# Memory products of two heads in either half of TensorE's rows, with the norm in the same stationary tile

## The chip, the cores and the metric

One core of a Trainium2 chip runs the whole program. The metric is device time in microseconds, from start to end of one execution; lower is better. The kernel before was run three times: 965.25, 966.20 and 967.39 us, median 966.2 us.

## What is computed

Three blocks follow one another: attention with a memory term, and two feed-forward blocks on its output. B = 4, H = 8, S = 576, D = 64; there are 2304 tokens of 512 features. The change concerns the memory term, `mem_ret` and `mem_norm`:

```python
def _attn_ref(q, k, v, M_prev, z_prev, beta):
    scores = scale * np.matmul(q, k.transpose(0, 1, 3, 2))
    ...
    local = np.matmul(a, v)
    q_p = phi(q)                      # where(x > 0, x, exp(x) - 1) + 1
    mem_ret = np.einsum('bhsd,bhde->bhse', q_p, M_prev)
    mem_norm = np.einsum('bhsd,bhd->bhs', q_p, z_prev)[..., None] + 1e-06
    mem_out = mem_ret / mem_norm
    g = 1.0 / (1.0 + np.exp(-beta))[None, :, None, None]
    return g * mem_out + (1 - g) * local

x = moe(attention)    # ((x @ w1) * (x @ w2)) @ w3 @ w_out
out = moe2(x)         # h = x @ w_in; (h * tanh(softplus(h))) @ w_out
```

## The kernel before

**Tasks.** Heads are taken in pairs. A `Task` is one pair of one batch, for one half (288 queries) of the sequence or for both. Batch 0 is split (eight tasks of one half each), batches 1 to 3 have four tasks of two halves each: 20 tasks, 32 halves. The first twelve (`AVF=12`) do the memory term and the product with V in float32, one `matmul` of which becomes two passes on TensorE. The last eight use float32r: a number is split into a high part and a low part and the product is the sum of three one-pass products, in the order of `HL = ((0, 0), (0, 1), (1, 0))`. So 16 halves are float32 and 16 are float32r.

**Stages of a task.** `load_qk` and `prep` bring K and Q of a head and split them (tile `QK`); `phi` makes the features of both heads, head 0 in partitions 0 to 63 and head 1 in 64 to 127 (tile `PH`). `load_vm` brings V and the memory. `SC` makes the scores on TensorE, finds their maxima with DVE and POOL; `SE` subtracts and takes the exponent. `MEM` makes the memory products, `AV` the products with V. At the end of the second head's `AV` the denominators are gathered by small DMAs through DRAM into `cp` so that 128 partitions can work on them, added to an epsilon, inverted, multiplied with the gate, sent back and broadcast into `Rr`, with which DVE multiplies `mnl`.

**The memory products before** (`MEM`, line 503). The stationary tile is 128 x 128, block-diagonal: M of head 0 in the upper left, M of head 1 in the lower right, so that one product over 128 rows gives both heads' outputs in 128 partitions. The two norm vectors are two more columns (`VZ = P + 2`) and a product of their own into a second PSUM bank, with 2 rows of output in float32 and 4 in float32r (high and low part of the vectors are columns beside one another; the two rows are added later). One ACT copy takes the outputs to `mnl`, one takes the norm rows to `R`:

```python
op("pe", cost, fm, r=rd, w=[pm])
act(HS, lambda qs=qs: mnl.tile[:, 0, qs], lambda pm=pm: pm.tile[:, 0:HS], [pm], [(mnl, (0, hf))], True)
op("pe", cost, fn, r=rd, w=[pn])
act(HS, lambda qs=qs, nz=nz: R.tile[0:nz, qs], ...)
```

**The norms of float32r tasks** (`AV`, line 647). The low rows of `R` go by a third DMA to DRAM, come back into a tile `cz`, and DVE adds them to `cp`.

**Who sets the order.** Every operation is recorded with an engine, a cost in ns and what it reads and writes (`op`, line 82). At the end `schedule` (line 111) lists them: each engine takes, when it is free in the planned time, the ready operation with the lowest key, for TensorE the place in the program (filler work 300 places later), for the others the longest remaining path. The result is one fixed order for each engine, which on the chip waits on semaphores only. Products of the first feed-forward block fill TensorE between attention steps (names `x`, `u`, `wA` to `wE`); the second feed-forward block comes after them. PSUM is eight banks, all with the name `g`. Lines 330, 333, 337, 339 and 347 are helpers (`mm`, `sub`, two forms of `act`, `tt`) and occur in rows of many tiles; DMAs are issued by the SP queue at line 327.

Of the kernel before, what the change touches and what calls it, by code (L numbers as in the profile page):

```python
# [14 lines left out]
P = 128  # L15
# [247 lines left out]
def kernel(  # L263
# [28 lines left out]
    VZ = P + 2  # L292
# [21 lines left out]
        "x": 10, "u": 4, "t": 8, "cp": 1, "cz": 2, **CFG.get("BUFS", {}),  # L314
# [126 lines left out]
    def load_vm(T):  # L441
        j = T.nj
        n = 2 * j * DV
        if T.f32:
            M = T.M = buf("M", [P, VZ])
            dma(lambda: Vf.tile[:, T.i % 2, 0:j], lambda: v[T.b, T.p, :, 0:j], 512 * n, w=[(Vf, T.i % 2)])
            dma(lambda: M.tile, lambda: mz[T.b, T.p], 66560, w=[M])
            return
        raw = buf("vr", [P, VZ + 2 * NJ * DV])
        mr = lambda: raw.tile[:, 0:VZ]  # L450
        vr = lambda: raw.tile[:, VZ:VZ + n].rearrange("p (j t d) -> p j t d", t=2, d=DV)
        dma(vr, lambda: v[T.b, T.p, :, 0:j], 512 * n, w=[(raw, 0)])
        dma(mr, lambda: mz[T.b, T.p], 66560, w=[(raw, 1)])

        M = T.M = buf("M", [P, 2 * VZ], F32R)
        act(VZ, lambda: M.tile[:, 0:VZ], mr, [(raw, 1)], [(M, 0)])
        for a, b, c in ((0, P, VZ + 2), (P, VZ, VZ)):
            lo(b - a, lambda a=a, b=b, c=c: M.tile[:, c:c + b - a], lambda a=a, b=b: mr()[:, a:b], lambda a=a, b=b: M.tile[:, a:b], [(raw, 1), (M, 0)], [(M, 1)])
# [44 lines left out]
    def MEM(T):  # L503
        T.mnl = buf("mnl", [P, 2, T.w])
        T.R = buf("R", [P, T.w])
        PH, mnl, R, M = T.PH, T.mnl, T.R, T.M
        for hf in T.hfs:
            pm, pn = gbuf(), gbuf()
            qs = T.qs(HS * hf, HS * hf + HS)
            if T.f32:  # L510
                rd, cost, nz = [PH, M], 2 * 248, 2
                fm = lambda pm=pm, qs=qs: mm(pm.tile[:, 0:HS], M.tile[:, 0:P], PH.tile[:, qs], True, True)
                fn = lambda pn=pn, qs=qs: mm(pn.tile[0:2, 0:HS], M.tile[:, P:VZ], PH.tile[:, qs], True, True)
            else:
                rd, cost, nz = [(z, y) for z in (PH, M) for y in range(2)], 3 * t_mm(HS), 4

                def fm(pm=pm, qs=qs):
                    for y, (a, b) in enumerate(HL):
                        mm(pm.tile[:, 0:HS], M.tile[:, (VZ + 2) * a:(VZ + 2) * a + P], PH.tile[:, b, qs], y == 0, y == 2)

                def fn(pn=pn, qs=qs):
                    mm(pn.tile[0:4, 0:HS], M.tile[:, P:VZ + 2], PH.tile[:, 0, qs], True, False)
                    mm(pn.tile[0:4, 0:HS], M.tile[:, P:VZ + 2], PH.tile[:, 1, qs], False, True)
# [80 lines left out]
    def AV(T, t):  # L604
# [35 lines left out]
        d0 = Buf(dram, [6, W], F32, f"d0_{W}", 2)  # L640
# [3 lines left out]
        dma(lambda: d0.tile[0:2], lambda: R.tile[0:2, :], 9216, r=[(R, (2, hf)) for hf in T.hfs], w=[(d0, 0)])  # L644
        dma(lambda: d0.tile[2:4], lambda: R.tile[32:65:32, :], 9216, r=[(R, (x, z)) for x in range(2) for z in range(len(T.outs))], w=[(d0, 1)])
        dma(lambda: cp.tile, lambda: d0.tile[0:4].rearrange("r (c e) -> (r c) e", e=ce), 9216, r=[(d0, 0), (d0, 1)], w=[(cp, 0)])
        if not T.f32:
            dma(lambda: d0.tile[4:6], lambda: R.tile[2:4, :], 9216, r=[(R, (2, hf)) for hf in T.hfs], w=[(d0, 2)])
            cz = buf("cz", [64, ce])
# [397 lines left out]
```

## Time and profile before

| | |
|---|---|
| median of three runs | 966.2 us |
| profiled execution: its time / its span | 965.84 us / 964.1 us |
| PE busy | 945.7 us (98%), 5440 matmul instructions |
| DVE busy | 725.8 us (75%), 1643 instructions |
| ACT busy | 607.0 us (63%), 1240 instructions |
| DMA queue | 31.3% of 16 engines |
| TensorE clock granted | 1.00, in every slice |

Busy time of PE includes the tail of each pipelined matmul, which lies beside the next one: how long a group of matmuls holds TensorE is read from its start to the start of what follows. The memory products stand between 6.7 and 431 us. From about 460 us on there is no attention left, only feed-forward products.

### The profile page before, as it was taken

Reading aid. Unit: us, or ns where it says so; the run is one execution under the profiler, and the core shown is the slowest. Engines: PE = TensorE matmul, PEld = TensorE weight load, DVE = VectorE, ACT = ScalarE, POOL = GpSimd, SP = SyncE. Lnnn points to the kernel's source line nnn. Section 1 sums busy time; section 2 is a strip of 40 time slices with the busy share of each in tenths; the row PEclk is TensorE's granted clock in tenths of the full one; section 3 lists DMA queues with packets and bytes.
Section 4 is the critical chain, followed back from the end, with each engine's and each line's share of the span. In section 5 each row is a group of like instructions: output and inputs, shape, how many; then the busy total and the mean of one; then the engine's idle time right before and its main releaser. Section 6 shows DMA issues by size and latency. Waiting matters only on the chain.

```text
span 964.1 us, 15222 instructions
## 1 busy us (share of the span) xinstructions
PE 945.7 (98%) x5440; PEld 808.9 (84%) x5440; DVE 725.8 (75%) x1643; ACT 607.0 (63%) x1240; POOL 86.4 (9%) x70
## 2 busy tenths in 40 slices
PE   6999999999999999999999999999999999999998
PEld 3454878778999999999999988888888888998997
DVE  7999999899999989896653987547554756565663
ACT  6677877778797778775433776446444544554653
POOL 1210012322222012120000000000000000000000
PEclk9999999999999999999999999999999999999999
DMA  9689655542433422302641740020002001100000
GB/s 351 215 246 303 201 167 153 156 141 82 142 98 91 151 75 83 107 26 83 203 153 49 228 167 1 1 81 7 1 1 83 1 0 32 46 1 17 34 1 33
DMA packets 48316, 96.62 MB, mean 100 GB/s; under 512 B 11024, under 2 KB 23344, under 8 KB 48240
## 3 DMA queue, kind: packets, MB, share of 16 engines
q1 hardware_dynamic: 48240, 95.64, 31.3%
q8 instruction: 43, 0.70, 0.3%
q14 instruction: 33, 0.27, 0.1%
HBM read 85.85 MB, written 9.77 MB: 99 GB/s over the span
## 4 chain that ended last, share of the span: by engine, by line
PE 67%; DVE 18%; ACT 6%; DMA 4%; issue 3%; SPq 1%; POOL 0%; DVEq 0%; ACTq 0%; POOLq 0%
PE g L330 67%; DVE t L347 4%; DVE QK L333 3%; DMA Rr<-d 2%; DVE e L333 1%; DVE e L347 1%; ACT t L339 1%; DVE mnl L347 1%; DVE g L560 1%; SPq L327 1%; DVE u L333 1%; DVE t L686 1%; ACT mnl L337 1%; DMA wA<-in_moe_w_out_dram 1%; ACT R L337 1%
## 5 line engine op out<-in xcount | busy, mean ns | idle before, releaser
L330 PE MATMUL g<-u,wA 128*128 128x288 f32 (+2 forms) x1008 | 162.6, 314 | 1.0 <-ACT u L337 0.6
L330 PEld LDWEIGHTS g<-u,wA 128*128 128x128 f32 x1008 | 147.2, 188 | 9.9 <-ACT u L337 1.0
L347 DVE TENSOR_TENSOR t<-g,t 128x288 f32<-128x288 f32 (+6 forms) x344 | 121.3, 380 | 22.2 <-PE g L330 14.4
L580 POOL PARTITION_ALL_REDUCE t<-t x64 | 85.8, 1342 | 352.0 <-DVE t L347 282.5
L330 PE MATMUL g<-x,wB 128*128 128x288 f32 x768 | 110.7, 298 | 0.8 <-DVE t L347 0.8
L330 PEld LDWEIGHTS g<-x,wB 128*128 128x128 f32 x768 | 104.7, 188 | 3.3 <-DVE t L347 1.4
L339 ACT ACTIVATE x<-x,two 128x512 f32<-128x512 f32 (+1 forms) x80 | 54.4, 680 | 70.8 <-DVE x L830 70.8
L339 ACT ACTIVATE x<-g 128x512 f32<-128x512 f32 (+1 forms) x98 | 55.0, 561 | 65.2 <-PE g L330 63.9
L330 PE MATMUL g<-e,V 128*65 128x320 f32 (+12 forms) x576 | 90.3, 303 | 1.9 <-ACT e L339 1.5
L833 DVE SCALAR_TENSOR_TENSOR x<-g,x 128x512 f32<-128x512 f32 (+1 forms) x80 | 51.0, 637 | 43.0 <-ACT x L339 42.6
L330 PEld LDWEIGHTS g<-e,V 128*65 128x65 f32 (+1 forms) x576 | 66.2, 136 | 20.3 <-ACT e L339 3.0
L829 DVE TENSOR_SCALAR x<-x 128x512 f32<-128x512 f32 (+1 forms) x80 | 31.8, 397 | 61.8 <-ACT x L339 60.0
L330 PE MATMUL g<-QK 128*128 128x320 f32 (+7 forms) x464 | 72.8, 298 | 5.2 <-DVE QK L333 5.1
L337 ACT CAST x<-x 128x512 fp32r<-128x512 f32 (+1 forms) x80 | 46.1, 577 | 50.4 <-DVE x L347 50.3
L330 PEld LDWEIGHTS g<-QK 128*128 128x128 f32 x464 | 64.0, 193 | 14.8 <-DVE QK L333 7.8
L333 DVE TENSOR_TENSOR t<-x 128x512 fp32r<-128x512 f32 (+1 forms) x80 | 50.9, 637 | 31.9 <-ACT x L337 30.6
L330 PE MATMUL g<-wB,wD 128*128 128x512 f32 x128 | 61.6, 619 | 3.9 <-DVE wD L686 2.1
L333 DVE TENSOR_TENSOR QK<-ld,QK 64x640 fp32r<-64x640 f32 (+1 forms) x80 | 61.7, 772 | 3.5 <-ACT QK L337 1.9
L330 PE MATMUL g<-x,wD 128*128 128x288 f32 x384 | 57.0, 298 | 0.0
L337 ACT COPY t<-g 128x288 f32<-128x288 f32 (+2 forms) x96 | 36.5, 394 | 32.5 <-PE g L330 24.7
L330 PE MATMUL g<-x,wE 128*128 128x288 f32 x384 | 56.2, 300 | 0.5 <-DVE e L347 0.4
L347 DVE TENSOR_TENSOR x<-x 128x512 f32<-128x512 f32 (+1 forms) x80 | 51.0, 637 | 6.0
(147 smaller groups left out, 1815.6 us busy)
## 6 DMA issues: line engine op xcount, KB each, us to landing
ld<-in_qk_dram SPq DMA_DIRECT2D x24, 608.0 KB
u<-in_moe_w_dram SPq DMA_DIRECT2D x26, 512.0 KB
Rr<-d SPq DMA_DIRECT2D x24, 288.0 KB
mnl<-in_moe_w_out_dram SPq DMA_DIRECT2D x11, 512.0 KB
mnl<-in_moe_w_in_dram SPq DMA_DIRECT2D x11, 512.0 KB
x2d<-t SPq DMA_DIRECT2D x16, 288.0 KB
out_dram<-x SPq DMA_DIRECT2D x18, 256.0 KB
wA<-in_moe_w_out_dram SPq DMA_DIRECT2D x8, 512.0 KB
```

Of the source, the lines that this page charges most:

```text
L327: op("sp", max(500, nbytes / 340.0), lambda: nc.sync.dma_start(out=dst(), in_=src()), r, w)
L330: nc.tensor.matmul(out=o, lhsT=lhsT, rhs=rhs, start=start, stop=stop)
L333: eng.tensor_tensor(out=o, in0=a, in1=b, op=ALU.subtract)
L337: op("act", t_act(n, psum), lambda: nc.scalar.copy(out=o(), in_=i()), r, w)
L339: op("act", t_act(n, psum), lambda: nc.scalar.activation(out=o(), in_=i(), func=func, **kw), r, w)
L347: op(eng, t_dve(n) if eng == "dve" else t_pool(n), lambda: e.tensor_tensor(out=o(), in0=a(), in1=b(), op=alu), r, w)
L560: nc.vector.tensor_tensor(out=o, in0=o, in1=mv, op=ALU.add)
L580: op("pool", 430 + 2.6 * (b - a), lambda mv=mv: nc.gpsimd.partition_all_reduce(mv(), mv(), P, bass_isa.ReduceOp.max), r=[(m, x)], w=[(m, x)])
L686: op("dve", t_dve(512), lambda: nc.vector.scalar_tensor_tensor(out=ci(), in0=ci(), scalar=3, in1=lw(), op0=ALU.logical_shift_left, op1=ALU ...
L829: op("dve", t_dve(n, True), lambda: nc.vector.tensor_scalar(out=w_(), in0=u(), scalar1=E20, scalar2=2.0, op0=ALU.min, op1=ALU.add), r=[ub_ ...
L833: op("dve", t_dve(n), lambda: nc.vector.scalar_tensor_tensor(out=u(), in0=hv(), scalar=2.0 ** -8, in1=u(), op0=ALU.mult, op1=ALU.mult), r= ...
```

## The change

The stationary tile of a head is now its own 64 partitions: 64 columns of M, and in the other 64 columns one column with its norm vector and zeros. Head 0 has M in columns 0 to 63 and z in column 64; head 1 has z in column 0 and M in columns 64 to 127. A half is one operation on TensorE with two PSUM banks, one for each head; head 0's product uses partitions 0 to 63 of `M` and `PH`, head 1's partitions 64 to 127, in turns over the passes. Outputs and norm of a head come out in one bank, and four ACT copies take them out: two of 64 x 288 to `mnl`, two of 1 x 288 to `R`, head 0's norm to row 0 and head 1's to row 96. In float32r tasks the low part of the norm is inside the three products, so the third DMA, `cz` and its addition are gone, as is the separate splitting of the two norm columns.

```diff
@@ load_vm
-            M = T.M = buf("M", [P, VZ])
+            M = T.M = buf("M", [P, P])
...
-        for a, b, c in ((0, P, VZ + 2), (P, VZ, VZ)):
-            lo(b - a, lambda a=a, b=b, c=c: M.tile[:, c:c + b - a], ...)
+        lo(P, lambda: M.tile[:, 1], mr, lambda: M.tile[:, 0], [(raw, 1), (M, 0)], [(M, 1)])
@@ MEM
-            pm, pn = gbuf(), gbuf()
+            pt = [gbuf(), gbuf()]
-            if T.f32:
-                rd, cost, nz = [PH, M], 2 * 248, 2
-                fm = lambda pm=pm, qs=qs: mm(pm.tile[:, 0:HS], M.tile[:, 0:P], PH.tile[:, qs], True, True)
-                fn = lambda pn=pn, qs=qs: mm(pn.tile[0:2, 0:HS], M.tile[:, P:VZ], PH.tile[:, qs], True, True)
-            else:
-                rd, cost, nz = [(z, y) for z in (PH, M) for y in range(2)], 3 * t_mm(HS), 4
...
-            op("pe", cost, fm, r=rd, w=[pm])
-            act(HS, lambda qs=qs: mnl.tile[:, 0, qs], lambda pm=pm: pm.tile[:, 0:HS], [pm], [(mnl, (0, hf))], True)
-            op("pe", cost, fn, r=rd, w=[pn])
-            act(HS, lambda qs=qs, nz=nz: R.tile[0:nz, qs], lambda pn=pn, nz=nz: pn.tile[0:nz, 0:HS], [pn], [(R, (2, hf))], True)
+            passes = [(None, None)] if T.f32 else HL
+            def fm(pt=pt, qs=qs):
+                for y, (a, b) in enumerate(passes):
+                    for t, r in enumerate(HALF):
+                        w, x = (M.tile[r], PH.tile[r, qs]) if T.f32 else (M.tile[r, a], PH.tile[r, b, qs])
+                        mm(pt[t].tile[:, 0:HS], w, x, y == 0, y == len(passes) - 1)
+            op("pe", 2 * 248 if T.f32 else 3 * t_mm(HS), fm, ..., w=pt)
+            for t, ps in enumerate(pt):
+                act(HS, lambda qs=qs, r=HALF[t]: mnl.tile[r, 0, qs], lambda ps=ps, r=HALF[t]: ps.tile[r, 0:HS], ...)
+                act(HS, lambda qs=qs, r=96 * t: R.tile[r:r + 1, qs], lambda ps=ps, r=64 - 64 * t: ps.tile[r:r + 1, 0:HS], ...)
@@ AV
-        dma(lambda: d0.tile[0:2], lambda: R.tile[0:2, :], 9216, ...)
+        dma(lambda: d0.tile[0:2], lambda: R.tile[0:97:96, :], 9216, ...)
...
-        if not T.f32:
-            dma(lambda: d0.tile[4:6], lambda: R.tile[2:4, :], 9216, ...)
-            cz = buf("cz", [64, ce])
-            dma(lambda: cz.tile, ..., 9216, r=[(d0, 2)], w=[cz])
-            op("dve", 90, lambda: nc.vector.tensor_tensor(out=cp.tile[0:64], in0=cp.tile[0:64], in1=cz.tile, op=ALU.add), ...)
```

The planned cost of a half on TensorE falls from two times 496 to 496 ns in float32, and from two times `3 * t_mm(HS)` to one in float32r, and ACT's planned work grows, so the fixed orders shift a little on every engine. They stay close: the attention steps keep their sequence, and the filler products before each of them are the same within a few.

On TensorE, in a float32 task, between filler products (`wB,wD`) and the next head's scores (`QK`; `e` with `V` are the products with V). Before:

```order
L330 MATMUL g<-wB,wD 128x512 x2
L330 MATMUL g<-PH,M 128x288
L330 MATMUL g<-PH,M 2x288
L330 MATMUL g<-QK 128x288 x2
L330 MATMUL g<-QK 128x160 x2
```

and with the change:

```order
L329 MATMUL g<-wB,wD 128x512 x2
L329 MATMUL g<-PH,M 128x288 x2
L329 MATMUL g<-QK 128x288 x2
L329 MATMUL g<-QK 128x160 x2
L329 MATMUL g<-QK 128x32 x2
```

The place is the same. In place of the outputs' product and the norms' product stand two products over 64 rows each, one for each head.

On TensorE, in a float32r task of two halves, between products of the feed-forward block (`u,wA`) and the next head's scores. Before:

```order
L330 MATMUL g<-u,wA 128x288 x48
L330 MATMUL g<-PH,M 128x288 x3
L330 MATMUL g<-PH,M 4x288 x2
L330 MATMUL g<-PH,M 128x288 x3
L330 MATMUL g<-PH,M 4x288 x2
L330 MATMUL g<-QK 128x256 x2
```

and with the change:

```order
L329 MATMUL g<-u,wA 128x288 x48
L329 MATMUL g<-PH,M 128x288 x12
L329 MATMUL g<-QK 128x256 x2
L329 MATMUL g<-QK 128x128 x2
L329 MATMUL g<-QK 128x320 x2
```

Ten products have become twelve, each over 64 rows, head 0 and head 1 in turns.

On ACT, the copies out of PSUM of one float32r task of two halves, with what stands behind them. Before:

```order
L337 COPY t<-g 128x288
L337 COPY mnl<-g 128x288
L337 COPY R<-g 4x288
L337 COPY mnl<-g 128x288
L337 COPY R<-g 4x288
L337 CAST PH<-t 128x576
L337 CAST M<-vr 128x130
L337 COPY t<-g 128x256
```

and with the change:

```order
L336 COPY mnl<-g 64x288
L336 COPY R<-g 1x288
L336 COPY mnl<-g 64x288
L336 COPY R<-g 1x288
L336 COPY mnl<-g 64x288
L336 COPY t<-g 128x256
L336 COPY R<-g 1x288
L336 COPY mnl<-g 64x288
L336 COPY R<-g 1x288
L336 COPY t<-g 128x320
L336 CAST QK<-ld 128x1216
L336 CAST PH<-t 128x576
```

Four copies have become eight. The copies of the next scores (`t<-g`) now stand between them, and the conversion of `QK` and that of `PH` for the next task behind them.

## Rows read from the trace of the kernel before

**Rows 1.** The page: span, busy time of each engine, chain of waits by engine.

```profile
span 964.1 us, 15222 instructions
PE 945.7 (98%) x5440; PEld 808.9 (84%) x5440; DVE 725.8 (75%) x1643; ACT 607.0 (63%) x1240; POOL 86.4 (9%) x70
...
PE 67%; DVE 18%; ACT 6%; DMA 4%; issue 3%; SPq 1%; POOL 0%; DVEq 0%; ACTq 0%; POOLq 0%
```

**Rows 2.** Four stretches: us, then busy us (x instructions) of each engine, clock, DMA.

```profile
0.00:50.00 50.00, 40.04 (x134) 20.52 (x135) 42.89 (x125) 31.79 (x62) 8.65 (x12) 1.00 0.79 280
50.00:215.00 165.00, 162.72 (x891) 118.28 (x889) 156.75 (x409) 125.05 (x274) 31.93 (x24) 1.00 0.63 196
215.00:450.00 235.00, 232.66 (x1779) 224.44 (x1779) 213.07 (x543) 183.09 (x424) 45.87 (x34) 1.00 0.32 95
450.00:964.00 514.00, 510.32 (x2643) 445.64 (x2641) 313.04 (x567) 267.02 (x482) 0.00 (x0) 1.00 0.17 54
```

**Rows 3.** The chain of waits from 50 to 215 us, by line.

```profile
by line: PE g L330 28.2%; DMA Rr<-d 8.0%; DVE QK L333 6.8%; DVE t L347 6.4%; issue 6.1%; DVE e L347 5.3%; DVE t L686 5.0%; DMA u<-in_moe_w_dram 2.7%; ACT e L339 2.2%; DVE u L333 2.1%; DVE wB L333 2.0%; DVE u L684 1.9%; ACT t L339 1.9%; DVE 
```

**Rows 4.** PE in order of time: start us, us, what; float32 MEM products.

```profile
27.74 1.23 PE L330 MATMUL g<-PH,M 128*128 128x288 f32 x4
28.89 0.88 PE L330 MATMUL g<-QK 128*128 128x288 f32 x6
29.62 1.04 PE L330 MATMUL g<-e,V 128*65 128x288 f32 x6
```

**Rows 5.** PE in order of time, the two MEM products of one half apart.

```profile
52.02 0.65 PE L330 MATMUL g<-PH,M 128*128 128x288 f32 x2
52.50 1.02 PE L330 MATMUL g<-wB,wD 128*128 128x512 f32 x2
53.45 0.65 PE L330 MATMUL g<-PH,M 128*2 128x288 f32 x2
54.03 0.89 PE L330 MATMUL g<-QK 128*128 128x288 f32 x6
```

**Rows 6.** PE in order of time, float32r MEM products: ten in a row, and apart.

```profile
315.63 1.48 PE L330 MATMUL g<-PH,M 128*128 128x288 f32 x10
316.95 1.12 PE L330 MATMUL g<-QK 128*128 128x256 f32 x8
...
282.77 0.56 PE L330 MATMUL g<-PH,M 128*128 128x288 f32 x3
283.17 1.76 PE L330 MATMUL g<-x,wB 128*128 128x288 f32 x12
284.77 0.43 PE L330 MATMUL g<-PH,M 128*4 128x288 f32 x2
285.03 1.76 PE L330 MATMUL g<-x,wB 128*128 128x288 f32 x12
```

**Rows 7.** Weight loads of six score products in order of time.

```profile
28.89 0.78 PEld L330 LDWEIGHTS g<-QK 128*128 128x128 f32 x6 [0.49 <-DVE QK L333]
```

**Rows 8.** ACT copies by shape: xcount | busy us, mean ns | idle before, releasers.

```profile
L337 ACT COPY mnl<-g 128x288 f32<-128x288 f32 x32 | 12.1, 393 | 3.2 <-DVE x L333 2.5 <-PE g L330 0.6
L337 ACT COPY mnl<-g 64x288 f32<-64x288 f32 x16 | 6.3, 392 | 1.5 <-PE g L330 1.3
L337 ACT COPY R<-g 1x288 f32<-1x288 f32 x16 | 6.3, 391 | 4.6 <-PE g L330 4.3
L337 ACT COPY R<-g 2x288 f32<-2x288 f32 x16 | 6.0, 382 | 1.1 <-DMA d<-R 1.1
L337 ACT COPY R<-g 4x288 f32<-4x288 f32 x16 | 6.0, 384 | 0.3 <-DMA d<-R 0.2
```

**Rows 9.** Tiles M, cz and R: instructions xcount, ns min/median/max, first and last start us, forms.

```profile
L333 DVE TENSOR_TENSOR M<-vr,M x16: 91/219/379, 221.6 to 403.4; 128x128 fp32r<-128x128 f32 x8, 128x2 fp32r<-128x2 f32 x8
...
L327 SPq DMA_DIRECT2D cz<-d x8: 471/478/549, 247.7 to 435.5; - x8
L651 DVE TENSOR_TENSOR cp<-cp,cz x8: 158/164/554, 270.7 to 457.3; 64x18 f32<-64x18 f32 x8
...
L327 SPq DMA_DIRECT2D d<-R x48: 238/308/581, 28.9 to 451.0; - x48
```

**Rows 10.** SP queue's waits, 215 to 470 us: in total, times, longest us.

```profile
SPq L327 <- DMA d<-R: 15.4, 8, 3.0
```

**Rows 11.** The chain of waits from 259 to 280 us in order of time.

```profile
260.11 0.68 DVE t L347 x2
260.81 0.63 ACT t L339
...
278.53 0.35 ACT e L337
278.91 1.05 DVE e L333
```

**Rows 12.** PE waits from 215 to 450 us: in total, times, longest us.

```profile
PE g L330 <- DVE t L347: 0.8, 1, 0.8
PE g L330 <- ACT u L337: 0.6, 1, 0.6
PE g L330 <- DVE u L333: 0.3, 1, 0.3
PE g L330 <- DVE e L333: 0.2, 1, 0.2
```

More of the change, by code (lines that the diff above doesn't have):

```diff
@@ L291 @@
     DV = D + 2
-    VZ = P + 2
     KQ = SK + S
@@ L507, in MEM @@
         for hf in T.hfs:
-            pm, pn = gbuf(), gbuf()
+            pt = [gbuf(), gbuf()]
             qs = T.qs(HS * hf, HS * hf + HS)
-            if T.f32:
-                rd, cost, nz = [PH, M], 2 * 248, 2
-                fm = lambda pm=pm, qs=qs: mm(pm.tile[:, 0:HS], M.tile[:, 0:P], PH.tile[:, qs], True, True)
-                fn = lambda pn=pn, qs=qs: mm(pn.tile[0:2, 0:HS], M.tile[:, P:VZ], PH.tile[:, qs], True, True)
-            else:
-                rd, cost, nz = [(z, y) for z in (PH, M) for y in range(2)], 3 * t_mm(HS), 4
[L517 to L523, printed above, removed]
-            op("pe", cost, fm, r=rd, w=[pm])
-            act(HS, lambda qs=qs: mnl.tile[:, 0, qs], lambda pm=pm: pm.tile[:, 0:HS], [pm], [(mnl, (0, hf))], True)
-            op("pe", cost, fn, r=rd, w=[pn])
-            act(HS, lambda qs=qs, nz=nz: R.tile[0:nz, qs], lambda pn=pn, nz=nz: pn.tile[0:nz, 0:HS], [pn], [(R, (2, hf))], True)
+            passes = [(None, None)] if T.f32 else HL
[4 more added lines that the diff above has]
+                        mm(pt[t].tile[:, 0:HS], w, x, y == 0, y == len(passes) - 1)
+            op("pe", 2 * 248 if T.f32 else 3 * t_mm(HS), fm, r=[PH, M] if T.f32 else [(z, y) for z in (PH, M) for y in range(2)], w=pt)
+            for t, ps in enumerate(pt):
+                act(HS, lambda qs=qs, r=HALF[t]: mnl.tile[r, 0, qs], lambda ps=ps, r=HALF[t]: ps.tile[r, 0:HS], [ps], [(mnl, (0, t, hf))], True)
+                act(HS, lambda qs=qs, r=96 * t: R.tile[r:r + 1, qs], lambda ps=ps, r=64 - 64 * t: ps.tile[r:r + 1, 0:HS], [ps], [(R, (2, t, hf))], True)
     def SC(T, t):
@@ L643, in AV @@
         rb = buf("Rr", [P, 2, W])
-        dma(lambda: d0.tile[0:2], lambda: R.tile[0:2, :], 9216, r=[(R, (2, hf)) for hf in T.hfs], w=[(d0, 0)])
+        dma(lambda: d0.tile[0:2], lambda: R.tile[0:97:96, :], 9216, r=[(R, (2, t, hf)) for t in range(2) for hf in T.hfs], w=[(d0, 0)])
         dma(lambda: d0.tile[2:4], lambda: R.tile[32:65:32, :], 9216, r=[(R, (x, z)) for x in range(2) for z in range(len(T.outs))], w=[(d0, 1)])
-        dma(lambda: cp.tile, lambda: d0.tile[0:4].rearrange("r (c e) -> (r c) e", e=ce), 9216, r=[(d0, 0), (d0, 1)], w=[(cp, 0)])
-        if not T.f32:
-            dma(lambda: d0.tile[4:6], lambda: R.tile[2:4, :], 9216, r=[(R, (2, hf)) for hf in T.hfs], w=[(d0, 2)])
-            cz = buf("cz", [64, ce])
-            dma(lambda: cz.tile, lambda: d0.tile[4:6].rearrange("r (c e) -> (r c) e", e=ce), 9216, r=[(d0, 2)], w=[cz])
-            op("dve", 90, lambda: nc.vector.tensor_tensor(out=cp.tile[0:64], in0=cp.tile[0:64], in1=cz.tile, op=ALU.add), r=[(cp, 0), cz], w=[(cp, 0)])
+        dma(lambda: cp.tile, lambda: d0.tile.rearrange("r (c e) -> (r c) e", e=ce), 9216, r=[(d0, 0), (d0, 1)], w=[(cp, 0)])
         cv = lambda: cp.tile
```

28 lines of the change are left out of this document (13 added, 15 removed).

## The prediction

> **What bounds the kernel now.** I read the page first. PE is busy for 945.7 of 964.1 us and has 67% of the chain of waits; DVE has 18%, ACT 6% [rows 1]. That looks like a kernel bound by TensorE alone, and for the last half it is. The stretches are not alike, though [rows 2]. From 450 us on there is no memory product, and nothing that the change touches. From 215 to 450 us, with the float32r tasks, PE is busy for 232.66 of 235 us, and DVE (213.07) and ACT (183.09) are close behind. From 50 to 215 us, with 13 of the 16 float32 halves, DVE is busy for 156.75 of 165 us, and the chain of that stretch [rows 3] has only 28.2% on PE: most of the time a PE that finished a product sooner would then wait longer for DVE or a DMA. So a microsecond of TensorE saved counts in full in the float32r stretch, where what follows is PE's own work, and for about 0.28 in the float32 stretch. ACT is the other thing to look at. It has 607.0 us of work, and 6% of 964.1 us, or 58 us, of the chain: 9.5% of its work lies on the chain. From 260.81 to 278.91 us it is the chain without a break, DVE before and after it [rows 11].
>
> **TensorE, float32 halves (16).** A half is four passes now. They start at 27.74 us and the scores behind them at 28.89 us: 1.15 us [rows 4]. The output product alone, with other 128-column work behind it, takes 52.50 - 52.02 = 0.48 us, so 0.24 us a pass; the norm product with its two columns takes 54.03 - 53.45 = 0.58 us [rows 5]. Four passes of 0.24 are 0.97 us; the 0.18 us that are left are two changes of the shape of the array's use, 0.09 us each. The Trainium skill, page "TensorEngine Tiling (Array Packing)", section "Tiling Modes", says that a change of tiling mode, not just of tile, drains TensorE; these rows agree, with 0.09 us for it.
>
> The change also has four passes, two for each head, and issues them as head 0, head 0, head 1, head 1. No row shows a product over 64 rows, so its cost is bounded. If the two halves of the rows don't work side by side, and the two changes of shape cost as before, it is 1.15 us again: nothing gained. If they do, the second pass of head 0 and the first of head 1 can overlap, no more, because a head's own passes follow each other. The first pass of head 1 then starts one weight load after the second of head 0. A weight load of 128 columns costs TensorE about 0.12 us where loads are what limits it: six score products hold it for 29.62 - 28.89 = 0.73 us [rows 4], with 960 columns in all that at 0.13 us per 288 (below) would take 0.44 us, and their loads follow one another without a gap [rows 7]. So 0.24 + 0.12 + 2 x 0.24 + 0.18 = 1.02 us, 0.13 less. The best bound is three passes and no change of shape, 0.72 us, 0.43 less. I take the middle one, 16 x 0.13 = 2.1 us off TensorE, because both of its prices stand in rows; at 0.28 it is worth **-0.6 us**.
>
> **TensorE, float32r halves (16).** Ten passes for two halves take 316.95 - 315.63 = 1.32 us, 0.132 us each, so 0.66 us a half. Apart, three outputs' passes take 0.40 us and two norm passes of four columns 0.26 us [rows 6]. Here the change to a few columns costs nothing, unlike in float32. Six passes come now instead of five. One after the other they are 6 x 0.132 = 0.79 us; in pairs with everything side by side 3 x 0.132 = 0.40 us; in pairs, with each pass waiting for its own weight load, 6 x 0.12 = 0.73 us. In the worst case two changes of shape of 0.09 us come on top of 0.79: 0.97 us. I take 0.73 us, for the loads are of 128 columns each, as in the row, and now there is one for every pass; no change of shape, as in these rows. That is 16 x 0.07 = **+1.1 us**, and the bounds are 16 x 0.26 = 4.2 us off and 16 x 0.31 = 5.0 us on.
>
> The Trainium skill, page "TensorE: Matmul & The Clock Gate", section "LDWEIGHTS (loading the stationary operand)", speaks against this change: a load's time goes by its columns, whatever the number of rows, so half a tile is no cheaper to load. The estimate from its formula is 107 ns a load, 0.64 us a half, and the sum would be 1.4 us lower.
>
> **ACT.** Each half has four copies instead of two: 64 more in all. They cost by columns, not by rows: 393 ns for 128 x 288, 392 for 64 x 288, 391 for 1 x 288, 382 and 384 for the old norm rows [rows 8]. So 64 x 0.39 = 25 us more work, half of it in either kind of task. At the share of ACT's work that lies on the chain, 9.5%, it is **+2.4 us**. The bounds are nothing, if PE and DVE cover it all, and the third rival below. Behind the copies on ACT's queue stand those of the next scores and the conversions of `QK` and `PH`, for which DVE waits.
>
> **DVE, DMAs, the rest.** In each of the eight float32r tasks a splitting of two columns (91 ns, the smallest of its row) and the addition of `cz` (158 ns) go [rows 9]: 8 x 0.25 = 2.0 us. DVE's share of the chain, 18% of 964.1 us, is 24% of its 725.8 us of work [rows 1]: **-0.5 us**. SP loses 16 issues, eight of 0.48 us to `cz` and eight of 0.31 us from `R` [rows 9], and at most eight waits of 15.4 us in all [rows 10]. I set it at nothing: `cp` still waits for its own way through DRAM, and SPq has 1% of the chain. The smaller `M` transfer, two columns less to convert, and two banks taken at once are nothing too: five passes of one half before and six now end within 0.1 us of each other.
>
> **The sum** is -0.6 + 1.1 + 2.4 - 0.5 = +2.4 us on the profiled execution's 965.84 us, 968.2 us. That execution was 0.4 us below the median of 966.2, so I expect a median near **968.4 us**. Less than 0.2%, 1.9 us, is not to be told from no change; this sum is just over that line.
>
> **Rivals.**
> 1. **The pairs run wholly side by side, weight loads too.** The Trainium skill, page "TensorEngine Tiling (Array Packing)", section "Tiling Modes", says that different tiles can execute weight loads and matmuls in parallel. In rows: 0.43 us less for a float32 half, 6.9 us in all, at 0.28 to 1 of it on the path; 4.2 us less for the float32r halves, in full. With 0.28: -1.9 - 4.2 + 2.4 - 0.5 = -4.2, **962 us**. For it: rows 6 show changes of shape that cost nothing in float32r. Against it: rows 4 and 7, where loads follow one another at 0.12 us even when the products are shorter.
> 2. **The halves of the rows work one after the other, and each change of shape drains.** Nothing is gained in float32, and 0.97 us replace 0.66 us in float32r: +5.0 + 2.4 - 0.5 = +6.9, **973 us**. This is the change not doing what it says. It decides as soon as head 1's pass starts a full 0.13 us after head 0's. For it: the 0.09 us of rows 5; against it: rows 6.
> 3. **ACT becomes the bound in the float32r stretch.** Its busy share there goes from 183.09 to 195.6 of 235 us, 83%. Where it is the whole chain, as in rows 11, a copy costs its full 0.39 us. With half of the 32 copies of that stretch there, 6.3 us, and the other 18.8 us at 9.5%: +8.1 - 0.5 + 0.5 from TensorE, some +8, **974 us**. It decides when PE starts to wait for ACT from 215 us on. Against it: PE's waits for ACT there are 0.6 us now [rows 12].
>
> **How the numbers follow.** I give the forecast 0.40 (its own range 966 to 971 us), the first rival 0.25, the second 0.22, the third 0.13. Faster by over 0.2% are the first rival and the forecast's tail below its range: 0.28. Within 0.2% is three quarters of what the forecast has below 969 us: 0.30. Slower is the rest of the forecast and two rivals: 0.42. The range takes in the first rival with some of its float32 gain, 960 us, and the third with a little more, 975 us.
>
> **What would show it.** In the profile after, matmul instructions should be 5456 (16 more), ACT's 1304, DVE's 1627, ACT busy near 632 us. A float32 half should take 1.0 us from its first pass to what follows, a float32r pair of halves 1.4 to 1.5 us for twelve passes: 0.8 us would be rival 1, 1.6 us or more rival 2. ACT waits of PE between 215 and 450 us over 3 us would be rival 3. The forecast is wrong if the time leaves 966 to 971 us, and its reasons are wrong if the float32r passes start in pairs or if ACT's added work leaves no trace in PE's waits.

## The result, and the profile after

The change takes 976.33 us (median of 4 runs, 975.2 to 977.11); beside it the kernel before took 966.8 us. The ratio is 1.0097, with a 95% interval of 1.0074 to 1.0119: 9.5 us slower, and outside the predicted range of 960 to 975 us. The profiled execution took 975.2 us.

The page of the changed kernel: span, engines, chain of waits.

```profile
span 973.4 us, 15335 instructions
...
PE 945.0 (97%) x5456; PEld 810.4 (83%) x5456; DVE 725.2 (75%) x1627; ACT 638.2 (66%) x1304; POOL 84.6 (9%) x70
...
PE 68%; ACT 12%; DVE 12%; DMA 4%; issue 2%; SPq 0%; DVEq 0%; ACTq 0%
```

The counts are those of the prediction (5456, 1304, 1627). ACT has 31.2 us more work than in [rows 1], where 25 were expected, and 12% of the chain instead of 6%.

Its four stretches, with the columns of [rows 2]:

```profile
0.00:50.00 50.00, 39.37 (x138) 20.76 (x139) 42.32 (x125) 33.65 (x66) 8.63 (x12) 1.00 0.77 278
50.00:215.00 165.00, 157.06 (x853) 116.57 (x853) 150.54 (x395) 133.12 (x289) 28.97 (x22) 0.98 0.61 188
215.00:450.00 235.00, 229.57 (x1737) 216.43 (x1735) 211.58 (x527) 195.77 (x451) 47.05 (x36) 0.99 0.33 95
450.00:973.00 523.00, 519.01 (x2733) 456.60 (x2732) 320.76 (x582) 275.67 (x501) 0.00 (x0) 1.00 0.17 56
```

In the first 450 us PE is busy 0.67, 5.66 and 3.09 us less than in [rows 2], 9.4 us together. Its work is not gone: the last stretch is 9 us longer and as full as before.

Its PE in order of time: a float32 half, and the twelve float32r products of two halves. Then its weight loads for that float32 half.

```profile
27.42 0.76 PE L329 MATMUL g<-PH,M 64*128 64x288 f32 x4
28.10 0.89 PE L329 MATMUL g<-QK 128*128 128x288 f32 x6
...
441.14 1.07 PE L329 MATMUL g<-PH,M 64*128 64x288 f32 x12
442.13 1.67 PE L329 MATMUL g<-QK 128*128 128x256 f32 x12
```

```profile
27.41 0.30 PEld L329 LDWEIGHTS g<-PH,M 64*128 64x128 f32 x4 [0.76 <-issue]
```

From its first pass to the scores a float32 half takes 0.68 us, where [rows 4] has 1.15. That is two pairs of 0.24 us and two changes of shape of 0.09 (0.66): both heads' products run beside each other, loads included, for the four loads take 0.30 us, less than four times the 0.12 us of [rows 4, 7]. Twelve float32r passes take 0.99 us, six times 0.132 and two changes of shape (0.97), where ten took 1.32 [rows 6]. If every half is like these, that is 16 x 0.47 + 8 x 0.33 = 10.2 us of TensorE time saved, an estimate. The kernel lost 9.5 us all the same.

What weight loads wait for from 50 to 215 us (in total, times, longest us), in the changed kernel and then in the kernel before:

```profile
PEld g L329 <- ACT mnl L336: 6.1, 10, 1.0
```

```profile
PEld g L330 <- ACT mnl L337: 0.7, 2, 0.5
```

These are products that need a PSUM bank which a copy to `mnl` has not yet left. The wait has grown from 0.7 to 6.1 us. Of the 6.1, 2.6 us are behind copies of 256 and 320 columns, those of the products with V, whose number did not change.

ACT in order of time, the copies of the last task's first half, in the changed kernel, and of both halves in the kernel before:

```profile
442.87 0.39 ACT L336 COPY mnl<-g 64x288 f32<-64x288 f32 x1
443.29 0.39 ACT L336 COPY R<-g 1x288 f32<-1x288 f32 x1
443.71 0.40 ACT L336 COPY mnl<-g 64x288 f32<-64x288 f32 x1
444.12 0.39 ACT L336 COPY R<-g 1x288 f32<-1x288 f32 x1
```

```profile
430.85 0.41 ACT L337 COPY mnl<-g 128x288 f32<-128x288 f32 x1
431.14 0.38 ACT L337 COPY R<-g 4x288 f32<-4x288 f32 x1
431.43 0.38 ACT L337 COPY mnl<-g 128x288 f32<-128x288 f32 x1
431.72 0.39 ACT L337 COPY R<-g 4x288 f32<-4x288 f32 x1
```

Each copy takes 0.39 us in either kernel. But before, one starts 0.29 us after the other, and in the change 0.41 to 0.42.

Last, the granted clock (the column ahead of the last two), in three windows of the changed kernel, and its PE around the two low ones:

```profile
178.00:179.30 1.30, 0.61 (x2) 0.16 (x2) 1.30 (x4) 0.65 (x1) 0.24 (x1) 1.00 0.16 62
179.30:186.10 6.80, 5.54 (x24) 5.54 (x24) 4.73 (x15) 6.50 (x16) 1.38 (x1) 0.50 0.49 146
373.90:377.30 3.40, 3.40 (x16) 3.40 (x16) 1.93 (x4) 1.39 (x4) 0.00 (x0) 0.50 0.02 7
```

```profile
176.98 1.63 PE L329 MATMUL g<-PH,M 64*128 64x288 f32 x4 [0.27 <-ACT mnl L336]
180.56 3.25 PE L329 MATMUL g<-x,wE 128*128 128x288 f32 x12 [1.94 <-DVE e L346]
...
372.02 5.78 PE L329 MATMUL g<-u,wA 128*128 128x288 f32 x27 [2.25 <-ACT u L336]
```

PE stood idle for 1.94 us behind DVE and for 2.25 us behind ACT. The clock was at 1.2 GHz, half, for 6.8 us from within the first wait on, and for 3.4 us from 1.9 us after the second. That takes at most half of 10.2, 5.1 us, less where PE would have waited anyway.

### The profile page after: what moved, and what is told of

Same layout as the page of the kernel before. It is cut to its first block, busy times and chain, and to the rows that moved or that the text cites. A ratio compares the mean times of both kernels' runs of the same rounds, so it can differ in the third digit from the quotient of the medians.

```text
span 973.4 us, 15335 instructions
## 1 busy us (share of the span) xinstructions
PE 945.0 (97%) x5456; PEld 810.4 (83%) x5456; DVE 725.2 (75%) x1627; ACT 638.2 (66%) x1304; POOL 84.6 (9%) x70
## 3 DMA queue, kind: packets, MB, share of 16 engines
q1 hardware_dynamic: 47568, 95.55, 31.2%
## 4 chain that ended last, share of the span: by engine, by line
PE 68%; ACT 12%; DVE 12%; DMA 4%; issue 2%; SPq 0%; DVEq 0%; ACTq 0%
PE g L329 68%; DMA Rr<-d 3%; DVE t L346 2%; ACT R L336 2%; ACT mnl L336 2%; ACT t L338 2%; DVE QK L332 2%; DVE mnl L346 1%; DVE e L346 1%; ACT QK L336 1%; ACT e L336 1%; ACT t L336 1%; DVE t L672 1%; DMA d<-cp 1%; ACT e L338 1%
## 5 line engine op out<-in xcount | busy, mean ns | idle before, releaser
L329 PE MATMUL g<-u,wA 128*128 128x288 f32 (+2 forms) x1008 | 164.6, 318 | 2.7 <-ACT u L336 2.3
L329 PEld LDWEIGHTS g<-u,wA 128*128 128x128 f32 x1008 | 149.6, 190 | 12.2 <-ACT u L336 2.5
L346 DVE TENSOR_TENSOR t<-g,t 128x320 f32<-128x320 f32 (+6 forms) x344 | 121.8, 383 | 21.6 <-PE g L329 10.7
L329 PE MATMUL g<-QK 128*128 128x320 f32 (+7 forms) x464 | 76.3, 304 | 8.8 <-DVE QK L332 5.5
L329 PEld LDWEIGHTS g<-QK 128*128 128x128 f32 x464 | 66.0, 196 | 17.5 <-DVE QK L332 8.7
L329 PEld LDWEIGHTS g<-x,wE 128*128 128x128 f32 x384 | 53.3, 193 | 3.9 <-DVE e L346 2.4
L336 ACT COPY R<-g 1x288 f32<-1x288 f32 (+2 forms) x128 | 50.0, 391 | 9.0 <-PE g L329 6.4
```

Of the source, the lines that this page charges most:

```text
L329: nc.tensor.matmul(out=o, lhsT=lhsT, rhs=rhs, start=start, stop=stop)
L336: op("act", t_act(n, psum), lambda: nc.scalar.copy(out=o(), in_=i()), r, w)
L346: op(eng, t_dve(n) if eng == "dve" else t_pool(n), lambda: e.tensor_tensor(out=o(), in0=a(), in1=b(), op=alu), r, w)
```

## The experiments

Theories. **A1:** ACT's time is short, and 64 more copies are too many. **A2:** it is where the copies stand, between a PSUM bank and its next product. **B:** the planner, told that a half costs TensorE half as much, made a worse order. All ratios are to the kernel before, in brackets the 95% interval; "above" and "below" compare with runs of the kernel before on the same chip, unless another kernel is named.

**Four copies with the old products.** The kernel before, with each of its copies doubled:

```diff
-            act(HS, lambda qs=qs: mnl.tile[:, 0, qs], lambda pm=pm: pm.tile[:, 0:HS], [pm], [(mnl, (0, hf))], True)
+            for t, r in enumerate(HALF):
+                act(HS, lambda qs=qs, r=r: mnl.tile[r, 0, qs], lambda pm=pm, r=r: pm.tile[r, 0:HS], ...)
...
+            act(HS, lambda qs=qs, nz=nz: R.tile[96:96 + nz, qs], lambda pn=pn, nz=nz: pn.tile[0:nz, 0:HS], ...)
...
```

> The kernel before, with its full-width products, but with four ACT copies a half instead of two, as in the change: mnl in two halves of the partitions, the norm rows twice. 64 copies of 0.39 us, 25 us, more on ACT, all out of PSUM; TensorE's work is as before. Theory A (ACT's added copies are the loss; the products side by side give back a part of it): slower than the change itself, since no TensorE time is saved: 976 to 986 us, with stalls of PE behind ACT. Theory B (the loss is the order that the planner makes with TensorE's halved costs): near the kernel before, 966 to 970 us.

980.86 us, 1.0141 [1.0121, 1.0162]: 14.0 us above. The copies alone cost more than the whole change. What its weight loads wait for copies to `mnl` from 50 to 215 us:

```profile
PEld g L330 <- ACT mnl L337: 2.6, 5, 1.0
```

That is less than half of the change's 6.1 us, in a kernel that lost more. So this wait does not measure the loss.

**As many copies, but inside SBUF.** The kernel before, with two copies in place after the two of a half:

```diff
+            act(HS, lambda qs=qs: mnl.tile[:, 0, qs], lambda qs=qs: mnl.tile[:, 0, qs], ...)
+            act(HS, lambda qs=qs, nz=nz: R.tile[0:nz, qs], lambda qs=qs, nz=nz: R.tile[0:nz, qs], ...)
```

> The kernel before with two more ACT copies a half that read and write SBUF (mnl and R onto themselves), behind the copies out of PSUM: the same number of added ACT instructions in the same places, about 0.4 us each, but no PSUM bank is held longer for them. Theory A1 (ACT's time is what is lacking): as much slower as with four copies out of PSUM, 976 us or more. Theory A2 (what hurts is that banks are held until more copies are through): at most 970 us.

967.91 us, 1.0009 [0.9996, 1.0021]. The pages of the two kernels, four copies and SBUF copies:

```profile
PE 952.3 (97%) x5440; PEld 811.5 (83%) x5440; DVE 729.1 (74%) x1643; ACT 637.3 (65%) x1304; POOL 85.4 (9%) x70
```

```profile
PE 945.6 (98%) x5440; PEld 808.6 (84%) x5440; DVE 726.7 (75%) x1643; ACT 627.7 (65%) x1304; POOL 87.3 (9%) x70
```

ACT has 1304 instructions in both and 30.3 and 20.7 us more work than before. In the second that costs 1 us. For A1 the other 10 us of ACT would have to cost 13 us; the hops, below, settle that.

**The change with two copies.** It leaves out head 1's outputs and head 0's norm:

```diff
-            for t, ps in enumerate(pt):
-                act(HS, ... mnl.tile[r, 0, qs], ... ps.tile[r, 0:HS], ...)
-                act(HS, ... R.tile[r:r + 1, qs], ... ps.tile[r:r + 1, 0:HS], ...)
+            act(HS, ... mnl.tile[:, 0, qs], lambda ps=pt[0]: ps.tile[:, 0:HS], ...)
+            act(HS, ... R.tile[0:1, qs], lambda ps=pt[1]: ps.tile[0:1, 0:HS], ...)
...
```

> The change with its products side by side, but two ACT copies a half: it leaves out the outputs of head 1 and the norm of head 0 (the 128 partitions of head 0's bank go to mnl with a scale, one norm row to R). TensorE's work is the change's, ACT's is that of the kernel before. Theory A: the copies were the loss, so what the products save is left: 956 to 964 us, the clock at 2.4 GHz throughout. Theory B: slow as the change, 972 to 978 us.

963.45 us, 0.9961 [0.9946, 0.9976]: 3.4 us below the kernel before and 12.9 below the change. With the first experiment this splits the result: the products side by side give 3 to 4 us, the four copies take 13 to 14.

```profile
PE 937.7 (98%) x5456; PEld 807.3 (84%) x5456; DVE 724.7 (76%) x1627; ACT 607.9 (63%) x1240; POOL 83.8 (9%) x70
```

PE is busy for 8.0 us less than before, so TensorE's saving is there once the copies are gone. In the change, with the same products, PE is busy for 945.0 us; the lower clock explains a part of that, and the rest stays open.

**The change with the old planned cost.**

```diff
-            op("pe", 2 * 248 if T.f32 else 3 * t_mm(HS), fm, ...)
+            op("pe", 4 * 248 if T.f32 else 6 * t_mm(HS), fm, ...)
```

> The change, with the planned TensorE cost of a half put back to what the two products were planned at before (twice the change's); nothing else. Only the fixed orders differ. Theory A: as the change within 3 us, 973 to 979 us. Theory B: most of the loss is gone, 964 to 970 us.

980.52 us, 1.0135 [1.0115, 1.0155]. It did not come back: B falls. But these are the change's instructions, and they take 4.2 us longer than in its own runs: a moved order alone can be worth some 4 us.

**One copy a bank, two hops inside SBUF.** The change, complete; each bank is emptied by one copy over 128 rows, and two ACT copies inside SBUF then bring the norm and head 1's outputs to their places (the gate rows change places with it):

```diff
+            act(HS, ... mnl.tile[:, 0, qs], lambda ps=pt[0]: ps.tile[:, 0:HS], ...)
+            act(HS, ... R.tile[:, qs], lambda ps=pt[1]: ps.tile[:, 0:HS], ...)
+            act(HS, ... R.tile[32:33, qs], ... mnl.tile[64:65, 0, qs], ...)
+            act(HS, ... mnl.tile[HALF[1], 0, qs], ... R.tile[HALF[1], qs], ...)
```

> The change with its products side by side, complete, but each of a half's two PSUM banks is freed by one copy of 128 x 288 (head 0's to mnl, head 1's to R); two more ACT copies then move the norm of head 0 and the outputs of head 1 inside SBUF. ACT has four copies a half as in the change, about 26 us more than before; a bank waits for one. Theory A2 (banks held until a second copy is through are the loss): as the run with two copies plus the 1 us that SBUF copies cost before, 962 to 967 us, faster than the change by 9 us or more. Theory A1 (ACT's time or the number of its copies): as the change, 973 to 979 us.

965.93 us, 0.9993 [0.9983, 1.0004], 10.4 us below the change.

```profile
PE 941.4 (98%) x5456; PEld 808.6 (84%) x5456; DVE 725.3 (75%) x1627; ACT 634.7 (66%) x1304; POOL 86.5 (9%) x70
```

ACT has the change's 1304 instructions and 634.7 of its 638.2 us. It is nearly the same load at another place, which is what A2 says. The wait from 50 to 215 us has hardly gone, though:

```profile
PEld g L329 <- ACT mnl L336: 4.8, 7, 2.0
```

**The hops on POOL.** The same, with the two SBUF copies on the engine that is nearly idle.

```diff
+            op("pool", t_pool(HS), ... nc.gpsimd.tensor_copy(out=R.tile[32:33, qs], in_=mnl.tile[64:65, 0, qs]), ...)
+            op("pool", t_pool(HS), ... nc.gpsimd.tensor_copy(out=mnl.tile[HALF[1], 0, qs], in_=R.tile[HALF[1], qs]), ...)
```

> As the run with two hops, with the two copies inside SBUF on POOL, which is 9% busy, instead of ACT. Theory A2: 961 to 967 us, near the two hops on ACT. Theory A1: faster than the two hops on ACT by as much as ACT's time is worth, 5 us or more, with that one near 975 us. A further possibility is that POOL's maxima, which the scores' exponents wait for, come later behind the copies: 968 to 974 us, with DVE waiting for POOL.

967.72 us, 1.002 [1.0005, 1.0034]. Taking 26 us off ACT again (608.5 us) gives nothing.

**Priority for the copies.** The change, with the four copies ahead of everything else that is ready on ACT.

```diff
-            o.key = ... else -o.tail + CFG["MIX"] * o.idx + (CFG["AB"] if o.bias else 0.0)
+            o.key = ... else -o.tail + CFG["MIX"] * o.idx + (CFG["AB"] if o.bias > 0 else -20000.0 if o.bias < 0 else 0.0)
...
+            held, rec.bias = rec.bias, -1
...
+            rec.bias = held
```

> The change, with its four copies a half taken by ACT before anything else that is ready in the planned order; nothing else. Same copies, same products. Theory A2: banks come free sooner, so a part of the loss goes: 966 to 972 us, and the time from a half's first pass to its last copy falls. Theory A1: no gain, 975 us or more, for ACT's other work is put back by the same amount.

980.74 us, 1.0142 [1.0119, 1.0166]. A miss. Averaged over the 32 banks of the float32r tasks, from a half's first pass to the end of the bank's last copy, a bank is held for 6.1 us here, for 5.5 in the change and 4.0 in the kernel before. Priority in the plan did not free the banks sooner on average, and the time rose by another 4 us with no instruction added.

**Banks held longer.** The kernel before; after both copies of a half, two copies of two elements each read the banks once more:

```diff
+            act(2, ... R.tile[96:97, qs.start:qs.start + 2], lambda pm=pm: pm.tile[0:1, 0:2], [pm, (mnl, (0, hf)), (R, (2, hf))], ...)
+            act(2, ... R.tile[96:97, qs.start + 2:qs.start + 4], lambda pn=pn: pn.tile[0:1, 0:2], [pn, (mnl, (0, hf)), (R, (2, hf))], ...)
...
```

> The kernel before, with two tiny ACT copies a half (2 elements of one row) that read the half's two banks after both full copies are through: some 64 x 0.1 to 0.2 us of ACT, under half of what the SBUF copies added, but each bank is held until both full copies and a tiny one have run. Theory A2: slower than before by 4 us or more, 971 to 980 us, though ACT has less to do than in the run with SBUF copies. Theory A1: at most 968 us.

972.82 us, 1.0071 [1.0054, 1.0088], with ACT busy for 616.6 us, 9.6 more. Less ACT work than the SBUF copies, six times their cost. The small copies hold up the DMA of the norm rows as well, which waits for them here; what that is worth is not separated, nor what of it is a moved order.

**One bank less.** The kernel before with one of its eight banks taken until the attention ends.

```diff
+    taken = gbuf()
+    op("dve", 70, lambda: nc.vector.memset(taken.tile[0:1, 0:2], 0.0), w=[taken])
...
+            op("dve", 70, lambda: nc.vector.tensor_copy(bt[0:1, 0:1], taken.tile[0:1, 0:1]), r=[taken, (T0.R, (1, 0))], w=[fb])
```

> The kernel before with one of its eight PSUM banks taken from the start of the tasks to the last product with V (one 2-element write, one 1-element read); nothing else. If banks are the scarce thing in the attention (theory A2), one bank in eight less costs much: slower by 8 us or more, 975 us and up, with PE waiting for ACT and DVE before 460 us. If they are not, within 2 us of before.

967.22 us, 1.0007 [0.9994, 1.0019]. A miss for A2 in its simple form: banks as such are not scarce. What is left of A2 is the particular product that needs a bank next, and its place in the fixed order; no run shows that.

**The hops in one kind of task.** The hops in the float32r tasks alone, then in the float32 tasks alone, the other kind as before:

```diff
+        T.new = not T.f32
...
+            if T.new:
...
+                act(HS, ... mnl.tile[:, 0, qs], lambda ps=pm: ps.tile[:, 0:HS], ...)
+                act(HS, ... R.tile[:, qs], lambda ps=pn: ps.tile[:, 0:HS], ...)
+                act(HS, ... R.tile[32:33, qs], ... mnl.tile[64:65, 0, qs], ...)
+                act(HS, ... mnl.tile[HALF[1], 0, qs], ... R.tile[HALF[1], qs], ...)
```

> Products side by side, with one copy out of PSUM for each bank and two hops inside SBUF, in the eight float32r tasks alone; the float32 tasks as in the kernel before. In the float32r stretch PE is the bound, so the 0.22 us a half that the pairs save should come through, less the hops: 16 x 0.22 = 3.5 us, less about 0.5 us: 962 to 965.5 us, and no fall of the clock before 215 us. If TensorE's savings do not come through even there: 966 to 968 us.

> The same in the twelve float32 tasks alone; the float32r tasks as in the kernel before. There DVE is the bound, so the 0.47 us a half that the pairs save turn into waits of PE: 965.5 to 968.5 us, with PE idle for some 5 us more before 230 us than in the kernel before, and perhaps a fall of the clock in one of the waits. If TensorE's savings did come through: 960 to 963 us.

964.76 us, 0.9975 [0.9963, 0.9988], and 972.41 us, 1.0058 [1.0038, 1.0078]. The second is a miss, and the two don't add up to 965.93. So the next four runs separate the kinds for the change itself, and the order from the work.

**The change in one kind of task.** Side by side with four copies in the float32 tasks alone, then in the float32r tasks alone:

```diff
+        T.new = T.f32
...
+            if T.new:
...
+                for t, ps in enumerate(pt):
+                    act(HS, ... mnl.tile[r, 0, qs], ... ps.tile[r, 0:HS], ...)
+                    act(HS, ... R.tile[r:r + 1, qs], ... ps.tile[r:r + 1, 0:HS], ...)
```

> The change in the float32 tasks alone (12 tasks, 16 halves, two heads side by side with four copies); the float32r tasks are those of the kernel before. If the 9.5 us come from more copies out of PSUM wherever they stand, both kinds of task pay for their 32 copies: this kernel and the one with the float32r tasks alone are each 3 to 7 us above the kernel before, and their differences add up to 9.5 us within 3 us. If the cost arises in the float32r stretch only, as the longest holds of the banks suggest, this kernel is within 2 us of before. If what counts is how the fixed order falls out, the two differences do not add up.

> The change in the float32r tasks alone, with its four copies; the float32 tasks are those of the kernel before. The same arrangement with one copy a bank and two hops gave 964.8 us. If the four copies out of PSUM are what costs, 969 to 974 us, the mean hold of a bank near 5 us and PE waits for ACT behind them; if the side by side products are the whole effect here, 963 to 966 us. The sum with the float32 half of the change is read as above.

975.07 us, 1.0086 [1.0067, 1.0104], and 967.26 us, 0.9998 [0.9987, 1.0009]: 7.9 and 0.1 us above, 8.0 together. The loss comes with the float32 tasks; in the float32r tasks the four copies and the products side by side come out level. With the hops in place of the four copies the same kinds were 6.0 us above and 1.7 below. So one copy a bank takes back 1.9 us in the float32 tasks and 1.7 in the float32r tasks, 3.6 together, and not the 10 us that it takes back when both kinds have it. From 50 to 215 us, the float32 kernel's window, and what its weight loads wait for there:

```profile
50.00:215.00 165.00, 156.96 (x857) 115.79 (x856) 151.31 (x399) 134.03 (x290) 29.00 (x22) 0.99 0.61 191
```

```profile
PEld g L330 <- ACT mnl L337: 5.9, 10, 1.0
```

And the same of the kernel with copies inside SBUF:

```profile
50.00:215.00 165.00, 162.19 (x893) 118.47 (x892) 157.74 (x413) 133.47 (x302) 32.35 (x24) 1.00 0.62 195
```

```profile
PEld g L330 <- ACT mnl L337: 2.3, 4, 0.9
```

ACT is as busy in the one as in the other, 134.03 and 133.47 us. PE is busy for 5.2 us less in the first, which waits 5.9 us for the copies and not 2.3. Part of the 5.2 is the saving itself, 0.47 us a half; and the first experiment, with 2.6 us of this wait, lost more than this kernel.

**The order alone.** The kernel before, every instruction as it was, planned with half the TensorE cost for a half; then also with the doubled ACT cost for its copies, as the change plans it:

```diff
-                rd, cost, nz = [PH, M], 2 * 248, 2
+                rd, cost, nz = [PH, M], 248, 2
...
-            act(HS, lambda qs=qs: mnl.tile[:, 0, qs], ...)
+            act(637, lambda qs=qs: mnl.tile[:, 0, qs], ...)
...
```

> The kernel before with the planned TensorE cost of a memory half cut to one half; every instruction is that of before, only their order moves. This shows how far a moved order alone shifts the time. If the order is worth little, 965 to 968 us. If the differences of several us between kernels with the same work (the hops in float32 tasks alone, the hops in both) come from the order, this kernel moves by 3 us or more as well.

> The kernel before, planned as if a half took half its time on TensorE and each of its two copies took ACT twice as long, as two copies each do in the change; the instructions are those of before. If the real extra copies cost the time, 965 to 969 us; if the order that a planner makes around them costs it, near 976 us, as the change.

964.94 us, 0.9976 [0.9966, 0.9987], and 965.26 us, 0.9983 [0.9972, 0.9995]. These two moved orders cost nothing; they gain 2 us. The old planned cost and the priority moved the change's own instructions by 4 us the other way. So differences of 2 to 4 us between kernels of this family can be the order's alone.

**The two products apart.** The float32 kernel from above, with each head's product an operation of its own, as before the change:

```diff
+                for t, ps in enumerate(pt):
+                    op("pe", 248, lambda ...: mm(ps.tile[:, 0:HS], M.tile[r, 0:P], PH.tile[r, qs], True, True), r=[PH, M], w=[ps])
```

> As the run with the change in the float32 tasks alone (975.07 us), but the two heads' products of a half are two operations, each with one bank, planned and placed apart as the two products of the kernel before; the four copies out of PSUM stay. If it is two banks taken at one moment, with four copies in a burst behind them, that holds up the float32 stretch, the time falls to 966 to 970 us. If it is the copies themselves, out of PSUM and on ACT in that stretch, it stays at 972 to 977 us, although the two products no longer run beside each other.

974.17 us, 1.0075 [1.0063, 1.0088], 7.2 us above. Its PE in order of time, a half whose products stayed together and one whose products came apart:

```profile
156.55 0.76 PE L330 MATMUL g<-PH,M 64*128 64x288 f32 x4
...
162.45 0.75 PE L330 MATMUL g<-PH,M 64*128 64x288 f32 x2
163.13 1.06 PE L330 MATMUL g<-u,wA 128*128 128x288 f32 x6
164.12 0.75 PE L330 MATMUL g<-PH,M 64*128 64x288 f32 x2
```

Only 6 of the 16 halves have their products apart, by 1.7 to 5.2 us; in the other ten the second starts within 0.35 us of the first. So the run does not rule out that two banks taken at one moment matter; with six halves apart the time moved by under 1 us.

**Two gains together.** Hops in the float32r tasks, and the cheaper plan for the float32 ones.

```diff
-                rd, cost, nz = [PH, M], 2 * 248, 2
+                rd, cost, nz = [PH, M], 248, 2
```

> Two gains put together: float32r tasks with products side by side, one copy a bank and two hops (964.76 us), and float32 tasks with the products of before, planned at half their cost (964.94 us with the plan of both kinds changed). If the two are independent, 962 to 963.5 us; if the moved order's gain arose in the float32r tasks, where this kernel has another plan already, 964 to 966 us.

966.23 us, 0.9989 [0.9977, 1.0001]. They don't add up.

**Other partitions.** The kernel before, the norm rows copied to partitions 96 and up, nothing else:

```diff
-            act(HS, lambda qs=qs, nz=nz: R.tile[0:nz, qs], ...)
+            act(HS, lambda qs=qs, nz=nz: R.tile[96:96 + nz, qs], ...)
...
```

> The kernel before with the norm rows copied to partitions 96 and up of R instead of 0 and up; number, shape and planned cost of every instruction stay. In the kernel before, copies from partition 0 to partition 0 start 0.29 us apart on ACT although each takes 0.39 (430.85, 431.14, 431.43, 431.72 us); in the change, whose copies read or write other partitions, they start 0.41 us apart. If the other partitions are what takes the overlap away, ACT's copies of a half start 0.39 to 0.42 us apart here too, ACT is busy for 611 to 615 us instead of 607 and the time rises by 1 to 4 us. If the missing overlap belongs to 64 rows instead of 128 or to the signals of the copies, the starts stay 0.29 us apart, ACT near 607 us and the time within 1.5 us of before.

967.82 us, 1.0018 [1.0007, 1.0028], ACT busy for 611.2 us. Its ACT in order of time, last task:

```profile
436.42 0.40 ACT L337 COPY mnl<-g 128x288 f32<-128x288 f32 x1
436.85 0.39 ACT L337 COPY R<-g 4x288 f32<-4x288 f32 x1
437.26 0.40 ACT L337 COPY mnl<-g 128x288 f32<-128x288 f32 x1
437.68 0.39 ACT L337 COPY R<-g 4x288 f32<-4x288 f32 x1
```

The starts are now 0.41 to 0.43 us apart instead of 0.29. Same shapes, same count: the partition that a copy goes to takes its overlap with its neighbours away. 32 such copies cost ACT 4.2 us and the kernel 1.7.

## Why the prediction was wrong

**TensorE, both terms: wrong, in the kernel's favour.** I took -0.6 and +1.1 us, from a second head's pass that starts one weight load later. In the halves shown above the passes start in pairs, within 0.02 us of each other, which the prediction named as a sign that its reasons are wrong. The pairs run wholly side by side, as the first rival had it; its 962 us were 14 us off because it took the same ACT term. The change with two copies gained 3.4 us, where that rival gave TensorE 6.1 (1.9 and 4.2) and my forecast a loss of 0.5. The Trainium skill, page "TensorEngine Tiling (Array Packing)", section "Tiling Modes", lets different tiles load weights and multiply in parallel; the 0.68 us half and its four loads in 0.30 us agree. The changes of shape that cost nothing with four columns cost 0.09 us with 64 rows in float32r as well.

**ACT: the step that failed.** "64 x 0.39 = 25 us more work ... at the share of ACT's work that lies on the chain, 9.5%, it is +2.4 us." The four copies measured 12.9 us (the change against itself with two) and 14.0 us (the kernel before with four). Two things are wrong in the term. Its size: 31.2 us, not 25, because the copies no longer overlap. The last experiment shows this for copies to partition 96, 4.2 us in 32 copies; that the change's copies from and to partition 64 lose it for the same reason is read from their starts alone. And, the larger part, its price: the average share priced a copy like any of ACT's work. The copies inside SBUF show that this is about right for work that nothing urgent waits for, 20.7 us for 1 us. That the copies out of PSUM are the cost is shown from both sides, by adding them and by taking them away. Why they are dear is argued: such a copy releases a bank, and a product of the fixed order stands behind it. The wait for it in the float32 stretch grew from 0.7 to 6.1 us in the change, but it is 2.6 us in the kernel with four copies, which lost 14.0, and 4.8 with the hops, which lost nothing.

**"Two banks taken at once are nothing":** not refuted, for taking six of the halves apart changed the time by 0.9 us. But I looked at when the banks are taken, and not at when they are given back, which now needs two copies for each.

**The third rival** named ACT, but for the float32r stretch, and there I trusted "PE's waits for ACT". By its own sign it came true: from 215 to 450 us PE waits 3.3 us for ACT, where its bound was 3.

```profile
PE g L329 <- ACT u L336: 2.3, 1, 2.3
PE g L329 <- ACT mnl L336: 0.7, 2, 0.5
PE g L329 <- ACT t L338: 0.3, 1, 0.3
```

Yet the change in float32r tasks alone costs 0.1 us, so that its 974 us lie near the result is luck, as it is for the second rival's 973. The loss comes with the float32 tasks, most of which lie where I gave PE's time a weight of 0.28, since it waited for DVE anyway. Of the 6.1 us there, 2.7 stand before scores (`QK`), and DVE's work follows those; that this is how they cost time is argued.

**DVE, DMAs:** 725.2 against 725.8 us busy, 0.6 us less where 2.0 were expected; no run isolates what it is worth.

**The clock** was not in the sum at all. Half clock for 10.2 us is worth up to 5.1 us here. No run isolates it; up to 450 us the change with two copies had one such spell of 3.4 us and the hops on POOL one of 6.8 us, and neither lost as the change did, while the four copies with the old products had one of 3.4 us and lost 14. So the loss does not rest on the clock; it comes along with the waits.

**What stays open.** Which part of the 13 us is the overlap, which the wait for the bank, and which ACT's own work that comes later behind the copies, such as the copies of the next scores; the last experiment suggests a few us for the first, not more, and no run separates the other two. Why the hops cost 6 us in the float32 tasks alone and nothing in both kinds; a moved order explains some 4 us at most in the runs here. Why holding banks longer costs 6 us and one bank less nothing: that it depends on which product comes next in the order is argued, not shown. Of the complete versions, hops in the float32r tasks alone (964.76 us) and the kernel before with a cheaper plan (964.94 us) are 0.25% below the kernel before, but since a moved order alone gives the second, I don't claim the first for its products.

## What to carry to other kernels

A copy is not priced by its engine's average share of the chain: 64 more inside SBUF cost 1 us here, 64 more out of PSUM 14. Look at what stands behind each, the product that needs its bank and the engine's own next work, and count the copies that a bank needs until it is free. A change that saves TensorE time by splitting an output over banks and partitions is worth a run with one copy a bank, from partition 0 to partition 0, and the rest moved inside SBUF; here that took some 10 us off the change, and left it level with the kernel before. And before a difference of 2 to 4 us is put down to an edit of a planned kernel, the same instructions in a moved order should be run.

## What the hardware showed that I had not expected

- Two products over 64 rows each run fully beside each other, weight loads too: 0.68 us for four float32 passes, changes of shape included, that would take 0.97 one after another without them.
- ACT copies of 288 columns take 0.39 us each, but from partition 0 to partition 0 they start 0.29 us apart, and 0.41 to 0.43 apart when one of them goes to partition 96.
- Around waits of PE of 1.94 and 2.25 us the granted clock was at 1.2 GHz for 6.8 and 3.4 us, in a kernel whose PE is busy for 97% of the span. In the kernel before with a cheaper plan, PE waits for 1.96 us at 177 us, and the clock is 1.00 from 165 to 200 us.
